# Two tiles of a fused attention and MLP kernel transposed by DMA instead of TensorE, and placed two or three slots sooner

## The chip, the cores and the metric

The kernel runs on one core of a Trainium2 chip. The metric is the device time of one execution in microseconds (us). The kernel before takes 292.99 us (median of 3 runs, 292.66 to 293.11).

## The reference

A linear attention with a normalisation per head, followed by an MLP with layer norm and a residual. B = 8 batches, H = 8 heads, S = 576 positions, D = 64, model width 512, hidden width 2048:

```
kv  = einsum('bhsd,bhse->bhde', k, v)
o   = einsum('bhsd,bhde->bhse', q, kv)
x   = o / sqrt(mean(o*o, -1) + 1e-6) * g_norm          # then heads side by side: (B, S, 512)
xn  = (x - mean(x)) / sqrt(var(x) + 1e-6) * g_ln
out = x + relu(xn @ w_ch1) @ w_ch2
```

## The kernel before: the parts that matter

Each batch has four main tiles of 128 positions, and a remainder of 64 positions that is paired with the next batch's. One tile passes through `o` (TensorE, product with kv), `sq` (ScalarE, squares), `red` (VectorE, the reduction that sums the squares of each head), the root (ScalarE), `y`, `x` and `xc` (VectorE: normalise, scale, centre), `var` (ScalarE) and `turn`, which gives the transposed `xT` that the first MLP product reads:

```python
def turn(self, on_pe):
    dst = self.blk[2][:, :, self.ts * 128:(self.ts + 1) * 128]
    if on_pe:
        tp = ps_m.tile([128, nK, 128], bf16, tag="misc", name="tp")
        for kk in range(nK):                                  # 4 transposes on TensorE
            nc.tensor.transpose(tp[:, kk, :], self.xc_t[:, kk * 128:(kk + 1) * 128], identity)
        nc.scalar.copy(dst, tp)                               # and a copy on ScalarE
    else:
        nc.sync.dma_start_transpose(dst, self.xc_t)           # one DMA on SP's queue
    ...
```

The MLP products of earlier batches run on TensorE, and the tiles of later batches are put between them at fixed places, called slots. A slot is four hidden blocks of MLP work for one tile (or as much for several), about 0.9 us. It is a place in the program order of every engine, not a moment in time:

```python
def plan_tile(s, make, turn_at, on_pe):
    ...                            # first(): o, sq, red;   second(): root, y, x, xc
    at(s, first)                   # third(): var;          fourth(): turn(on_pe)
    at(s + 2, second)
    at(s + 6, third)
    at(turn_at, fourth)
```

Batch 2, which the change touches, and the later batches:

```python
at(36, lambda: kv_of(2))
at(36.5, lambda: turn_q_dma(2))
for j, s, tn in ((0, 46, 53), (1, 51, 58), (2, 55, 63), (3, 59, 68)):
    plan_tile(s, lambda j=j: main_tile(2, j), tn, True)
plan_tile(62, lambda: rem_tile(1), 69, False)
...
for b in range(3, B):
    s = 32 * b
    ...                                                 # load_batch(b), gated on qt of b - 1
    d = -41 if b == 3 else -45
    at(s + d, lambda b=b: kv_of(b))
    at(s + d + 1.7, lambda b=b: turn_q_dma(b))          # q_p copy on VectorE, then qt by DMA on SP
    for j in range(J):
        o = s + d + (10 if b == 3 else 12) + 5 * j
        plan_tile(o, lambda b=b, j=j: main_tile(b, j), o + 6, False)
    ...
```

Slots 48 to 63 are the second MLP product of batch 1, with an output store on SP after every fourth slot. Slots 64 to 71 are the first MLP product of batch 2 for its tiles 0 and 1, slots 72 to 79 for tiles 2 and 3. So `xT` of tiles 0 and 1 is needed at slot 64 and that of tiles 2 and 3 at slot 72. Tile 0 of batch 3 has its `o` at slot 65 and needs `qt` of batch 3, the transposed queries, by then.

Of the kernel before, what the change touches and what calls it, by code (L numbers as in the profile page):

```python
# [14 lines left out]
def kernel(  # L15
# [183 lines left out]
    def turn_q_dma(b):  # L199
        q_p = kv_in.tile([128, JJ, H, D], bf16, tag="qp", bufs=2)  # L200
        nc.vector.tensor_copy(q_p.rearrange("p j h d -> p h j d"), q_in[b % NB])
        q_t = qt_pool.tile([128, JJ, HP, 128], bf16, tag="qt", name="qt")
        nc.sync.dma_start_transpose(
            q_t.rearrange("p j hp t -> p (j hp) t"), q_p.rearrange("p j h d -> p (j h d)"))
        qts[b] = q_t
# [35 lines left out]
    def new_block(n, bufs):  # L241
        x_blk = xpool.tile([128, 4, Dm], f32, tag=f"x{n}", bufs=bufs, name="x_blk")
        st_blk = xpool.tile([128, 3, 4], f32, tag=f"st{n}", bufs=bufs, name="st_blk")
        xT_blk = xpool.tile([128, nK, 512], bf16, tag=f"xT{n}", bufs=bufs, name="xT_blk")
        return x_blk, st_blk, xT_blk
# [98 lines left out]
    def main_tile(b, j, pool=None, tag="ops"):  # L344
        q_t, kvp = qts[b], held[b]
        if b not in blks:
            blks[b] = new_block("main", 3)
        return Tile([(slice(0, 128), lambda hp: q_t[:, j, hp, :], kvp)], blks[b], j, pool, tag)

    def rem_tile(b):  # L350
        mms = []
        for half, bb in enumerate((b - 1, b)):
            qt, kp = qts.pop(bb), held.pop(bb)
            mms.append((slice(half * 64, (half + 1) * 64),
                        lambda hp, qt=qt: qt[:, J, hp, :64], kp))
        if "rem" not in blks:
            blks["rem"] = new_block("rem", 1)
        return Tile(mms, blks["rem"], b // 2)

    def plan_tile(s, make, turn_at, on_pe):  # L360
        box = []

        def first():
            t = make()
            box.append(t)
            t.o()
            t.sq()
            t.red()

        def second():  # L370
            t = box[0]
            t.y()
            t.x()
            t.xc()

        def third():
            box[0].var()

        def fourth():
            box[0].turn(on_pe)  # L380

        at(s, first)
# [3 lines that stand above are left out]
# [72 lines left out]
    def at(slot, fn):  # L458
        agenda.setdefault(int(slot), []).append((slot, fn))
# [145 lines left out]

    at(36, lambda: kv_of(2))
    at(36.5, lambda: turn_q_dma(2))
    for j, s, tn in ((0, 46, 53), (1, 51, 58), (2, 55, 63), (3, 59, 68)):
        plan_tile(s, lambda j=j: main_tile(2, j), tn, True)
    plan_tile(62, lambda: rem_tile(1), 69, False)  # L610
    at(78, lambda: rstd_of(2))

    for b in range(3, B):
        s = 32 * b
# [69 lines left out]
```

## Time and profile before

| what | value | view |
|---|---|---|
| time, median | 292.99 us | timed runs |
| span of the profiled execution | 291.4 us | page |
| PE busy | 283.4 us, 97% | page, part 1 |
| PE busy from 90 to 93 us | 2.73 of 3.00 us | table of windows |
| PE weight loads waiting for qt of batches 4 to 7 | 2.0 us in 4 waits | view of waits |

First the head of the page of before: busy time, share and number of instructions of TensorE's products (PE) and of its weight loads (PEld).

```profile
span 291.4 us, 5801 instructions
PE 283.4 (97%) x2320; PEld 159.1 (55%) x2320; DVE 150.7 (52%) x335; ACT 154.7 (53%) x341; POOL 41.9 (14%) x68
```

TensorE bounds the kernel. Next, windows of before: the window's length, then busy time of PE, PEld, DVE, ACT and POOL (with numbers of instructions), the granted clock, the DMA share and GB/s.

```profile
63.00:66.00 3.00, 3.00 (x57) 3.00 (x55) 0.04 (x1) 2.26 (x6) 2.87 (x5) 1.00 0.49 50
81.00:84.00 3.00, 3.00 (x27) 1.80 (x27) 2.86 (x8) 1.18 (x2) 0.98 (x2) 1.00 0.90 178
87.00:90.00 3.00, 3.00 (x34) 2.72 (x33) 2.49 (x5) 2.15 (x7) 1.06 (x2) 1.00 1.31 217
90.00:93.00 3.00, 2.73 (x26) 2.30 (x24) 1.79 (x5) 3.00 (x9) 0.00 (x0) 1.00 1.39 189
```

VectorE has nothing to do from 63 to 66 us (0.04 us) and is nearly full near 81 to 84 us. TensorE has one hole in this stretch, after 90 us. The timeline of before (start, duration, engine, line, operation, and in brackets the idle time before it and what ended it) shows where the hole comes from. It also has the rows that later distances start and end at: the last transpose of batch 1, which I use as a mark, the `o` of the third tile of batch 3, and the last output operation. `p` is an MLP product in PSUM, the memory that TensorE writes to; `m` is ScalarE's eviction of it, which frees that part of PSUM (a bank) for the next product.

```profile
61.15 0.39 PE L337 MATMUL tp<-identity,xc 128*128 128x128 bf16 x4
76.55 0.82 DVE L201 COPY q_p<-q_in 128x2560 bf16<-128x2560 bf16 x1
77.86 3.18 SPq L203 DMA_TRANSPOSE qt<-q_p  x1
84.30 0.39 PE L260 MATMUL o_ps<-kv_pack,qt 128*128 128x128 bf16 x4
...
87.42 0.68 DVE L287 TENSOR_REDUCE ss<-sq 128x8 f32<-128x512 f32 x1
88.13 0.30 ACT L297 ACTIVATE rms<-ss,eps_sb 128x8 f32<-128x8 f32 x1 [0.85 <-DVE ss L287]
88.34 0.58 ACT L405 ACTIVATE m<-p 128x512 bf16<-128x512 f32 x1
...
90.00 1.08 ACT L405 ACTIVATE m<-p 128x512 bf16<-128x512 f32 x2
90.64 3.68 PE L402 MATMUL p<-xT_blk,w_sb 128*128 128x256 bf16 x32 [0.27 <-ACT m L405]
94.16 0.39 PE L260 MATMUL o_ps<-kv_pack,qt 128*128 128x128 bf16 x4
...
287.90 0.35 DVE L423 SCALAR_TENSOR_TENSOR o_sb<-p,rstd,x_blk 128x128 f32<-128x128 f32 x1 [0.54 <-PE p L418]
```

Read it backwards. TensorE stops at 90.6 us because ScalarE has not yet emptied a PSUM bank (`m` at 90.00). ScalarE had stood idle for 0.85 us until 88.13 behind a root, waiting for the reduction at 87.42; the eviction at 88.34 comes after that root in program order and ran after it, though the last matmul of its product ended at 87.30 in the timeline (87.03 + 0.27). That reduction began 3.1 us after the `o` of its tile (at 84.30), since VectorE had a backlog (it is busy without a pause from 84.22 us, with outputs and the work of earlier tiles).

Last, from the view of waits and the source view of before: the waits on qt, and the time that the DMA transposes of a tile's `xT` take from issue to landing (all data arrived).

```profile
PEld L260 <- DMA qt<-q_p: 2.0, 4, 0.6
...
L341 SPq DMA_TRANSPOSE xT_blk<-xc x24: 1189/1216/1365, 87.5 to 227.9; - x24
...
DMA to landing us min/median/max: 2.4/3.5/9.1
```

A DMA turn occupies SP for 1.2 us and lands after 2.4 us at best, 9.1 at worst.

### The profile page before, as it was taken

What the parts mean: (1) busy time and instruction counts of PE and PEld (TensorE: products, weight loads), DVE (VectorE), ACT (ScalarE), POOL (GpSimd) and SP (SyncE); (2) the same over time, 40 slices, a digit from 0 to 9 for tenths busy, and PEclk for the clock granted to TensorE, in tenths of its full rate; (3) what the DMA queues carried; (4) which work ended last, traced back from release to release, by engine and by line L of the source; (5) the groups of instructions that cost most, each with busy time, mean ns of one, the idle gap of its engine ahead of it and who ended that gap; (6) DMA issues with size and microseconds to landing.
All of it is one profiled execution on the core that took longest, in us unless ns stands there. A gap on an engine that the chain in (4) does not pass through costs nothing.

```text
span 291.4 us, 5801 instructions
## 1 busy us (share of the span) xinstructions
PE 283.4 (97%) x2320; PEld 159.1 (55%) x2320; DVE 150.7 (52%) x335; ACT 154.7 (53%) x341; POOL 41.9 (14%) x68
## 2 busy tenths in 40 slices
PE   8889999999999999999999999999999999999995
PEld 3579755995578654444444444444444444444444
DVE  5776028836996893765266936752678200220022
ACT  3457755885569931882189408920894066016500
POOL 8522520032050003200220023000000000000000
PEclk9999999999999999999999999999999999999999
DMA  7999999469789818993999279939202510131033
GB/s 212 202 206 205 198 204 217 102 100 192 144 141 201 110 41 153 217 162 65 159 192 140 56 145 192 165 64 167 58 18 55 109 36 0 38 78 30 0 74 72
DMA packets 63290, 35.84 MB, mean 123 GB/s; under 512 B 30748, under 2 KB 58268, under 8 KB 63264
## 3 DMA queue, kind: packets, MB, share of 16 engines
q0 software_dynamic: 28016, 17.76, 43.8%
q1 hardware_dynamic: 34736, 16.99, 29.7%
q10 hardware_dynamic: 512, 0.72, 0.8%
q8 instruction: 18, 0.29, 0.4%
q14 instruction: 8, 0.07, 0.1%
HBM read 36.71 MB, written 9.44 MB: 158 GB/s over the span
## 4 chain that ended last, share of the span: by engine, by line
PE 83%; DMA 6%; DVE 6%; ACT 2%; issue 1%; POOL 1%; POOLq 0%
PE p L402 40%; PE p L418 36%; DMA qt<-q_p 4%; PE o_ps L260 3%; DMA q_in<-in_q_dram 2%; PE kv_ps L235 2%; DVE ss L287 1%; DVE x_blk L311 1%; DVE y L292 1%; DVE o_sb L423 1%; PE tp L183 1%; ACT m L405 1%; PE p L196 1%; ACT xT_blk L339 1%; PE tp L337 0%
## 5 line engine op out<-in xcount | busy, mean ns | idle before, releaser
L402 PE MATMUL p<-xT_blk,w_sb 128*128 128x128 bf16 (+2 forms) x1024 | 132.0, 286 | 0.5 <-ACT m L405 0.3
L418 PE MATMUL p<-w_sb,m 128*128 128x512 bf16 (+2 forms) x608 | 130.2, 368 | 0.0
L405 ACT ACTIVATE m<-p 128x512 bf16<-128x512 f32 x144 | 85.2, 597 | 45.3 <-PE p L402 43.5
L402 PEld LDWEIGHTS <-w_sb 128*128 128x128 bf16 x1024 | 78.6, 98 | 45.5 <-issue 1.1
L418 PEld LDWEIGHTS <-m 128*128 128x128 bf16 x608 | 56.6, 98 | 60.3
L423 DVE SCALAR_TENSOR_TENSOR o_sb<-p,rstd,x_blk 128x512 f32<-128x512 f32 (+2 forms) x38 | 27.3, 719 | 44.2 <-PE p L418 41.5
L266 ACT ACTIVATE sq<-o_ps 128x512 f32<-128x512 f32 x34 | 20.2, 595 | 38.9 <-PE o_ps L260 38.9
L287 DVE TENSOR_REDUCE ss<-sq 128x8 f32<-128x512 f32 x34 | 23.2, 682 | 19.8 <-ACT sq L266 19.8
L329 ACT ACTIVATE dev<-x_blk,st_blk 128x512 f32<-128x512 f32 x36 | 25.8, 718 | 6.2 <-DVE st_blk L315 6.1
L321 DVE SCALAR_TENSOR_TENSOR xc<-x_blk,st_blk,g_ln_sb 128x512 bf16<-128x512 f32 x34 | 25.6, 752 | 1.2
L292 DVE TENSOR_TENSOR y<-o_ps,inv 128x512 f32<-128x512 f32 x34 | 23.5, 691 | 2.6
L311 DVE SCALAR_TENSOR_TENSOR x_blk<-y,g_norm_sb 128x512 f32<-128x512 f32 x34 | 23.5, 691 | 1.2
L411 DVE RECIPROCAL rstd<-rstd 128x4 f32<-128x4 f32 x9 | 1.6, 174 | 39.3 <-ACT rstd L410 39.3
L304 DVE RECIPROCAL inv<-rms 128x8 f32<-128x8 f32 x36 | 7.2, 200 | 22.5 <-ACT rms L297 22.4
L98 POOL COPY gate<-qt 1x1 bf16<-1x1 bf16 x5 | 1.4, 287 | 115.3 <-DMA qt<-q_p 115.3
L297 ACT ACTIVATE rms<-ss,eps_sb 128x8 f32<-128x8 f32 x36 | 10.8, 300 | 7.8 <-DVE ss L287 7.1
L260 PEld LDWEIGHTS <-qt 128*128 128x128 bf16 (+1 forms) x152 | 9.7, 100 | 8.4 <-DMA qt<-q_p 2.0
L260 PE MATMUL o_ps<-kv_pack,qt 128*128 128x128 bf16 (+1 forms) x152 | 13.3, 221 | 0.4 <-DVE qt L191 0.2
L196 PE MATMUL p<-fill_sb 128*128 128x512 bf16 x28 | 8.6, 465 | 1.2 <-DVE eps_sb L137 1.2
L339 ACT COPY xT_blk<-tp 128x512 bf16<-128x512 bf16 x10 | 5.8, 579 | 2.3 <-PE tp L337 2.3
L329 ACT ACTIVATION_READ_ACCUMULATOR dev<-x_blk,st_blk 128x1 f32 x36 | 7.0, 193 | 0.0
L238 ACT CAST kv_pack<-kv_ps 64x256 bf16<-64x256 f32 x7 | 2.6, 365 | 7.9 <-PE kv_ps L235 7.8
(79 smaller groups left out, 119.0 us busy)
## 6 DMA issues: line engine op xcount, KB each, us to landing
out_dram<-o_sb SPq DMA_DIRECT2D x70, 128.0 KB, 2.5
w_sb<-in_moe_w_ch_dram POOLq DMA_DIRECT2D x8, 512.0 KB, 13.8
k_in<-in_k_dram POOLq DMA_DIRECT2D x7, 320.0 KB, 5.1
v_in<-in_v_dram POOLq DMA_DIRECT2D x7, 320.0 KB, 8.8
q_in<-in_q_dram POOLq DMA_DIRECT2D x7, 320.0 KB, 12.1
q_in<-in_q_dram POOLq DMA_DIRECT2D x8, 256.0 KB, 12.4
k_in<-in_k_dram POOLq DMA_DIRECT2D x7, 256.0 KB, 6.5
v_in<-in_v_dram POOLq DMA_DIRECT2D x7, 256.0 KB, 11.0
```

The source lines that it names most:

```text
L196: nc.tensor.matmul(p1, lhsT=fill_sb[:, :128], rhs=fill_sb, start=True, stop=True)
L260: nc.tensor.matmul(flat[rows, hp * 128:(hp + 1) * 128], lhsT=lhsT_of(hp), rhs=kvp[:, hp, :], start=True, stop=True)
L266: nc.scalar.activation(self.sq_t, self.o_ps, func=AF.Square)
L287: nc.vector.tensor_reduce(self.ss, self.sq_t, axis=AX.X, op=ALU.add)
L292: nc.vector.tensor_mul(self.y_t, self.o_ps, self.inv().to_broadcast([128, H, D]))
L311: nc.vector.scalar_tensor_tensor(x_blk[:, ts].rearrange("p (h d) -> p h d", h=H), in0=self.y_t, scalar=1.0, in1=g_norm_sb.to_broadcast([12 ...
L321: nc.vector.scalar_tensor_tensor(self.xc_t, in0=x_blk[:, self.ts], scalar=st[:, 1, self.ts:self.ts + 1], in1=g_ln_sb, op0=ALU.add, op1=ALU ...
L329: nc.scalar.activation(dev, x_blk[:, ts], func=AF.Square, bias=st[:, 1, ts:ts + 1], accum_out=st[:, 2, ts:ts + 1])
L402: nc.tensor.matmul(p1[:, i, :], lhsT=w1_sb[:, kk, de * 128:(de + 1) * 128], rhs=blk[2][:, kk, sl], start=(kk == 0), stop=(kk == nK - 1))
L405: nc.scalar.activation(m1[:, de0:de0 + per, sl], p1, func=AF.Relu)
L418: nc.tensor.matmul(p2[:, c0:c1], lhsT=m1s[b][:, de, ts * 128:(ts + 1) * 128], rhs=w2_sb[:, de, c0:c1], start=(de == 0), stop=(de == nDe - 1))
L423: nc.vector.scalar_tensor_tensor(o_sb[:, c0:c1], in0=p2[:, c0:c1], scalar=rstds[b][:, ts:ts + 1], in1=blks[b][0][:, ts, c0:c1], op0=ALU.mu ...
```

## The change

The intent is to take eight transposes off TensorE, which bounds the kernel, and to start tiles 0 and 1 earlier so that the longer way of a DMA turn still ends before slot 64.

```diff
-    for j, s, tn in ((0, 46, 53), (1, 51, 58), (2, 55, 63), (3, 59, 68)):
-        plan_tile(s, lambda j=j: main_tile(2, j), tn, True)
+    for j, s, tn in ((0, 44, 50), (1, 48, 54), (2, 53, 61), (3, 58, 67)):
+        plan_tile(s, lambda j=j: main_tile(2, j), tn, j > 1)
```

Tiles 2 and 3 stay on TensorE, but they too move by two slots and one slot.

## The prediction

> **What bounds the kernel now.** TensorE. The profile's first part has PE busy 283.4 us of 291.4 (97%), and the chain of waits is 83% PE. The change acts from 63 to 91 us. In the table of 3 us windows PE is full there but for 90 to 93 us (2.73 of 3.00). The wait view names that hole: PE waited 0.3 us for ScalarE's `m` eviction. The chain explains it backwards: ScalarE sat 0.85 us behind a root that needed `red` of the remainder tile, late because VectorE had been backed up since about 73 us (2.9 of 3 us busy in most windows from 69 to 87).
>
> **What it removes.** For tiles 0 and 1: 4 transposes each, 0.22 us of PE per tile in the chain (0.45 us together, on the critical engine), and two ScalarE copies of 0.58 us, off the chain.
>
> **What it adds.** Two DMA transposes on SP's queue: 1.2 us of issue each; the 24 present ones land after 2.4 us alone, 7 to 9 us beside batch loads (source view). Even 9 us is in time: I expect xc of tile 0 at about 69 us and of tile 1 at 73, xT by 76 to 79; slot 64 starts at 83.
>
> **What it moves.** Tile 0 goes from slot 46 to 44 (about 63.2 us; qt landed at 62.6, so no wait), tile 1 from 51 to 48, tile 2 from 55 to 53, tile 3 by one. VectorE starts where it was idle (0.04 of 3 us in 63 to 66). But its order changes: y, x, xc of tile 2 (2.5 us) now precede output 1 of batch 1 and the q_p copy of batch 3, and the reductions are followed at once by the root they wait for (some 0.5 us exposed each time). I estimate that q_p starts at 77.5 to 78 instead of 76.55. Its DMA transpose (5.0 us to landing, 83.0 before) then lands at about 84.0; slot 65 needs it at 83.8 (before 84.2). So a new PE wait of 0 to 0.5 us on qt of batch 3 is likely.
>
> Second collision: the transposes share DMA engines with the loads of batch 3 (k and v landed by 72.2, q by 75.4). The Trainium skill, page "DMA: Bandwidth & Descriptors", section "Issuing engines are not separate DMA queues", says DMAs of all issuers run on the same 16 engines and interleave; the trace agrees (7.8 us against 2.4 to landing). One tile is about 1 us of all engines (estimate from the queue shares); kv of batch 3 needs v at 73.55: slack 1.3 us, so 0 to 0.3 us of PE wait.
>
> **Sum.** -0.45 (PE transposes), -0.1 to -0.3 (the hole at 90.6 shrinks), +0.25 (qt), +0.05 (v): net about -0.3 us. After 95 us PE order drives the kernel, so what is gained stays; the four later waits on qt (2.0 us together) remain.
>
> Predicted 292.65 us, 8 in 10 between 292.0 and 293.4. Chances: faster by over 2% 0.01, within 2% 0.98, slower by over 2% 0.01.
>
> **What would show it.** Right: 32 PE transposes of xc instead of 40, 26 DMA transposes of xT; PE busy about 0.5 us less; slot 64 about 0.4 us earlier; q_p of batch 3 about 1 us later and a new short PE wait on qt near 84 us; the hole at 90.6 smaller. Wrong: PE waiting for xT at slot 64, for kv inputs near 73.5, or for a PSUM bank held by a late output near 79.
>
> **What would make it wrong.** Transposes slowing the loads more than estimated; VectorE's backlog growing, so that qt comes over 1 us late and later loads follow; or VectorE keeping up, so that the whole 0.7 us is kept.

## The result, and the profile after

The new kernel takes 292.48 us (median of 4 runs, 292.22 to 292.58) against 293.01 us for before (292.66 to 293.11, 4 runs, three of them those above). The ratio is 0.9983, with a 95% interval of 0.9965 to 1.0000. Ratios here are the mean time of one kernel's runs over that of the other's in the same rounds, so they are not quite the ratio of the medians quoted.

The same views of the new kernel, first the head of its page:

```profile
span 290.8 us, 5789 instructions
PE 283.6 (98%) x2312; PEld 158.6 (55%) x2312; DVE 151.0 (52%) x335; ACT 154.1 (53%) x339; POOL 41.3 (14%) x68
```

There are eight products and eight weight loads fewer, and two ScalarE copies fewer. PE busy is nevertheless not smaller (283.6 against 283.4 us): among other differences, the warm-up products at the start of the kernel, which the change does not touch, show 9.4 us against 8.6. The time of the weight loads fell, 159.1 to 158.6 us. Then the windows of the new kernel:

```profile
63.00:66.00 3.00, 3.00 (x58) 3.00 (x56) 0.69 (x1) 2.52 (x7) 2.99 (x5) 1.00 0.53 51
81.00:84.00 3.00, 2.97 (x25) 1.59 (x20) 2.65 (x8) 1.64 (x5) 0.00 (x0) 1.00 1.06 199
87.00:90.00 3.00, 3.00 (x32) 2.70 (x31) 2.36 (x6) 3.00 (x8) 2.07 (x4) 1.00 1.24 156
90.00:93.00 3.00, 3.00 (x30) 2.69 (x28) 1.60 (x4) 2.83 (x8) 0.00 (x0) 1.00 1.49 141
```

The hole after 90 us is gone, and a small one has appeared in 81 to 84 us (2.97). The timeline of the new kernel says what it is:

```profile
61.06 0.39 PE L337 MATMUL tp<-identity,xc 128*128 128x128 bf16 x4
...
69.02 1.20 SPq L341 DMA_TRANSPOSE xT_blk<-xc  x1
74.53 2.33 SPq L341 DMA_TRANSPOSE xT_blk<-xc  x1
77.57 0.82 DVE L201 COPY q_p<-q_in 128x2560 bf16<-128x2560 bf16 x1
78.89 3.25 SPq L203 DMA_TRANSPOSE qt<-q_p  x1
83.94 0.23 PEld L260 LDWEIGHTS <-qt 128*128 128x128 bf16 x4 [0.31 <-DMA qt<-q_p]
86.30 0.68 DVE L287 TENSOR_REDUCE ss<-sq 128x8 f32<-128x512 f32 x1
87.09 0.31 ACT L297 ACTIVATE rms<-ss,eps_sb 128x8 f32<-128x8 f32 x1
93.36 0.39 PE L260 MATMUL o_ps<-kv_pack,qt 128*128 128x128 bf16 x4
...
287.42 0.35 DVE L423 SCALAR_TENSOR_TENSOR o_sb<-p,rstd,x_blk 128x128 f32<-128x128 f32 x1 [0.54 <-PE p L418]
```

The q_p copy of batch 3 starts 1.0 us later than in before, its transpose is issued 1.0 us later, and at 83.94 us TensorE waits for it: a wait that before did not have. (The ends of products are modelled, so the window shows little of it; but that `o` follows the first product of slot 64 by 1.07 us, against 0.88 in before.) The reduction of tile 0 of batch 3 starts at 86.30 us instead of 87.42, and the root that had held ScalarE back now runs at 87.09 with no idle time ahead of it. From the view of waits and the source view of the new kernel:

```profile
PEld L260 <- DMA qt<-q_p: 2.3, 4, 1.0
...
L341 SPq DMA_TRANSPOSE xT_blk<-xc x26: 1189/1199/2358, 69.0 to 227.9; - x26
```

**Measuring against a mark.** The start of the kernel scatters from run to run: the mark stands at 61.15 us in before and at 61.06 in the new kernel, and among all profiled runs it lies between 60.71 and 62.16. (The latest, in dma_only, goes with a granted clock of 0.89 from 15 to 30 us, where before has 1.00; after the mark it has 1.00 too.) The code up to the mark is the same in all of them. I therefore count from the mark. The third tile's `o` of batch 3 comes 33.01 us after it in before (94.16 - 61.15) and 32.30 us after it in the new kernel (93.36 - 61.06): a lead of 0.71 us. At the end of the kernel (start of the last output operation) the distances are 226.75 and 226.36 us, so only 0.39 us of the lead is left. The rest of the 0.5 us between the medians is not accounted for by the stretch after the mark; it lies within the scatter of the timed runs.

### The profile page after: what moved, and what is told of

It is laid out like the page before. It is cut to its first block, busy times and chain, and to the rows that moved or that the text cites. A ratio compares the mean times of both kernels' runs of the same rounds, so it can differ in the third digit from the quotient of the medians. Undisturbed runs are those within 1.5% of the kernel's fastest.

```text
span 290.8 us, 5789 instructions
## 1 busy us (share of the span) xinstructions
PE 283.6 (98%) x2312; PEld 158.6 (55%) x2312; DVE 151.0 (52%) x335; ACT 154.1 (53%) x339; POOL 41.3 (14%) x68
## 4 chain that ended last, share of the span: by engine, by line
PE 89%; DMA 6%; ACT 1%; DVE 1%; issue 1%; POOL 1%; POOLq 0%
PE p L402 42%; PE p L418 39%; DMA qt<-q_p 4%; PE o_ps L260 3%; DMA q_in<-in_q_dram 2%; PE kv_ps L235 2%; PE tp L183 1%; PE p L196 1%; PE tp L337 1%; ACT sq L266 0%; PE tp L170 0%; POOL v_in L126 0%; PE o_half L500 0%; ACT xT_blk L542 0%; ACT m L405 0%
## 5 line engine op out<-in xcount | busy, mean ns | idle before, releaser
L196 PE MATMUL p<-fill_sb 128*128 128x512 bf16 x28 | 9.4, 501 | 1.2 <-DVE eps_sb L137 1.2
L196 PEld LDWEIGHTS <-fill_sb 128*128 128x128 bf16 x28 | 3.2, 121 | 6.1 <-issue 3.9
```

The source lines that it names most:

```text
L196: nc.tensor.matmul(p1, lhsT=fill_sb[:, :128], rhs=fill_sb, start=True, stop=True)
```

## The experiments

**Theory.** Two separate terms make the lead: 0.45 us of TensorE transposes removed, and the hole near 90 us, which closes because VectorE starts earlier. Two things take part of it back: the new wait on qt of batch 3 and the later waits on qt. **Rivals.** The hole closed because ScalarE has two copies fewer, or because of the DMA turns; or there is one term only; or the result is noise.

All twelve runs gave correct results, and each is "same" as before at 2%. Distances are from the mark in the profiled execution. "Slot 64" is the first product of batch 2's MLP, "o(3,2)" the third tile's `o` of batch 3. The medians come from four jobs, in which before had 293.01, 292.78, 293.18 and 292.94 us.

| kernel | slot 64 | o(3,2) | last output | median us (job) |
|---|---|---|---|---|
| before | 22.27 | 33.01 | 226.75 | 293.01 (1) |
| new kernel | 21.82 | 32.30 | 226.36 | 292.48 (1) |
| after_again | 21.82 | 32.30 | 226.37 | 292.41 (3) |
| shift_only | 22.27 | 32.55 | 226.46 | 292.57 (2) |
| dma_only | 22.05 | 32.50 | 226.59 | 292.64 (2) |
| slack3 | 21.83 | 32.10 | 226.16 | 292.24 (2) |
| before_slack3 | 22.26 | 32.54 | 226.35 | 292.38 (3) |
| slack_all | 21.82 | 32.10 | 225.12 | 291.44 (2) |
| slack_all_b | 21.82 | 32.10 | 225.13 | 291.61 (4) |
| before_slack_all | 22.27 | 32.55 | 225.57 | 291.75 (3) |
| before_slack_all_b | 22.27 | 32.55 | 225.57 | 291.71 (4) |
| slack_all_t2 | 21.60 | 31.87 | 224.90 | 291.43 (3) |
| after_t2 | 21.60 | 32.30 | 225.66 | 291.84 (4) |
| slack_all_t23 | 21.60 | 38.30 | 231.42 | 298.32 (4) |

Three kernels were profiled twice (the new one and the two with slack throughout), and their distances agree within 0.01 us. That is why these columns can carry differences of 0.2 us and the timed medians can't. Before itself was profiled once.

### after_again: is the first result noise?

No edit; the new kernel once more.

> The new kernel itself, beside the others of this call. Theory: 0.4 to 0.6 us under before, as at first (0.53 us), and in the trace TensorE is 0.6 to 0.8 us ahead of before at the o product of the third tile of batch 3 (near 94 us), counted from the transpose of the last tile of batch 1, with 0.1 to 0.4 us of it given back at the later waits on qt. Rival (the first result was noise): within 0.15 us of before.

It took 292.41 us (292.28 to 292.72, 6 runs) against 293.18 (292.56 to 294.57, 11 runs), ratio 0.9978 (0.9963 to 0.9992). The median difference of 0.77 us is above the expected range, because before scattered upwards in this job: two of its eleven runs, at 294.00 and 294.57 us, show a lower mean clock, 0.994; without them its median is 292.97 and the difference 0.56 us. The trace is the same as the first within 0.01 us at both ends: a lead of 0.71 us at o(3,2), of which 0.33 us is lost by the end. The noise rival falls.

### shift_only: the new slots, all turns on TensorE

The tiles stand as in the new kernel; the turns of tiles 0 and 1 are one and three slots later than there.

```diff
-    for j, s, tn in ((0, 44, 50), (1, 48, 54), (2, 53, 61), (3, 58, 67)):
-        plan_tile(s, lambda j=j: main_tile(2, j), tn, j > 1)
+    for j, s, tn in ((0, 44, 51), (1, 48, 57), (2, 53, 61), (3, 58, 67)):
+        plan_tile(s, lambda j=j: main_tile(2, j), tn, True)
```

> The slots of the new kernel, but all four tiles of batch 2 turned on TensorE (40 transposes of xc, as before). Theory (the gain is two terms: 0.45 us of TensorE transposes removed by the DMA turns, and 0.45 us of a TensorE stop near 90 us that goes because VectorE's work on batch 2 starts 2 us sooner): the stop near 90 us is gone here as well, TensorE reaches slot 65 about 0.45 us later than in the new kernel and so does not wait for qt of batch 3 (landing near 84.0), and the time is about 0.3 to 0.5 us under before, within 0.2 us of the new kernel. Rival (ScalarE's two freed copies, or the DMA turns themselves, removed the stop): the stop of 0.3 us or more near 90 us stays, and the time equals before within 0.15 us.

292.57 us, ratio to before 0.9988 (0.9976 to 1.0000). Slot 64 comes exactly where it does in before (22.27), since no TensorE work is removed, and o(3,2) comes 0.46 us sooner. The hole is gone and there is no wait on qt at slot 65:

```profile
90.00:93.00 3.00, 3.00 (x30) 2.70 (x28) 1.70 (x4) 2.84 (x8) 0.00 (x0) 1.00 1.32 182
```

So the shift alone closes the hole, with all of ScalarE's copies kept, and the hole is worth 0.46 us. (The shift also moves tile 3's copy one slot forward, from behind the root to ahead of it. That this is not what closes the hole is shown by before_slack3, where no copy changes its slot.) The timed median lies 0.21 us under before, less than the expected 0.3 to 0.5; the trace's end, 0.29 us under before, has the same order.

### dma_only: the old slots, tiles 0 and 1 turned by DMA

```diff
-    for j, s, tn in ((0, 44, 50), (1, 48, 54), (2, 53, 61), (3, 58, 67)):
+    for j, s, tn in ((0, 46, 53), (1, 51, 58), (2, 55, 63), (3, 59, 68)):
         plan_tile(s, lambda j=j: main_tile(2, j), tn, j > 1)
```

> The slots of before, tiles 0 and 1 turned by DMA. Theory: tile 1's turn now stands on SP behind the 640 KB transpose of batch 3 (issue until about 81.1 us), so its xT lands at 84 to 86 us while slot 64 needs it at about 83.0: TensorE waits 1 to 3 us there, and the time is 0.3 to 2 us above before. The shift is thus needed for the DMA turn. Rival (a DMA turn needs no head start; its only effect is 0.45 us less TensorE work): no wait at slot 64, and the time is 0.4 us under before.

A miss: I expected 0.3 to 2 us above before, and the time equals that of before. It took 292.64 us (292.35 to 293.95; the profiled run is the slowest), ratio 0.9999 (0.9983 to 1.0014). Tile 1's transpose did stand behind that of batch 3 on SP, until 81.6 us, but landed 2.5 us later. The chain of waits of this run has the transpose, and its timeline the weight loads of slot 64:

```profile
81.64 2.53 DMA xT_blk<-xc
...
84.22 0.75 PEld L402 LDWEIGHTS <-w_sb 128*128 128x128 bf16 x7 [0.35 <-issue]
```

Slot 64 comes at 22.05 us instead of 21.82 in the new kernel: a wait of 0.23 us, not of 1 to 3. The chain passes through this DMA, which lands at 84.17 us, just before the weight loads go on; the label "issue" in the line above only says that the timeline found no releaser. I had taken the long landings beside batch loads for the rule; here the loads of batch 3 had landed and those of batch 4 had not begun. At slot 64 the head start is worth 0.23 us, no more. The hole near 90 us shrank to 0.15 us in the weight loads (0.45 in before) without the shift; TensorE came to it later by the wait at slot 64, so the two effects are mixed in this run, and it does not tell how the hole depends on the copies.

### before_slack3: only the hole's cause

Before, with tile 0 of batch 3 one slot later and nothing else.

```diff
-            o = s + d + (10 if b == 3 else 12) + 5 * j
+            o = s + d + (10 if b == 3 else 12) + 5 * j + (b == 3 and j == 0)
```

> The kernel before, with tile 0 of batch 3 one slot later and nothing else. There is no wait on qt of batch 3 to remove in before. Theory (the TensorE stop near 90.6 us comes from ScalarE standing behind the root of that tile, whose reduction VectorE's backlog delays to 88.1 us): in program order the root now comes after four more products, so fewer evictions stand behind it, the stop falls from 0.45 us to under 0.15 us and TensorE is 0.3 to 0.5 us ahead of before near 95 us. Rival (the stop comes from ScalarE's xT copies or its load in general): the stop stays at 0.3 us or more, and the time equals before within 0.15 us.

292.38 us against 293.18, ratio 0.9979 (0.9964 to 0.9994), about as fast as the new kernel without any of its change. The lead at o(3,2) is 0.47 us. Its windows:

```profile
87.00:90.00 3.00, 3.00 (x33) 2.71 (x31) 1.62 (x5) 3.00 (x8) 0.55 (x1) 1.00 1.30 229
90.00:93.00 3.00, 3.00 (x30) 2.70 (x28) 2.46 (x7) 2.88 (x8) 0.00 (x0) 1.00 1.36 183
```

ScalarE is full from 87 to 90 us (2.15 of 3 in before), TensorE has no hole. The number of copies is that of before. So the hole was one instruction in the wrong place of ScalarE's program order: a root placed ahead of evictions while its input was still behind VectorE's backlog. The edit moves all of that tile's work by a slot; that it was the root is read from the traces (0.85 us of idle time before it in before, none here). Either moving the tile later or clearing the backlog sooner (shift_only) closes the hole.

### slack3: the new wait on qt of batch 3

The same edit, applied to the new kernel.

> The new kernel with tile 0 of batch 3 one slot (0.9 us) later, so that qt of batch 3 has landed. Theory: the wait of 0.31 us that the trace shows on qt near 84 us goes, TensorE reaches 95 us about 0.2 us sooner, and the time is 0.1 to 0.25 us under the new kernel, if nothing gives it back at the later waits on qt. Rival (the wait costs nothing, later waits take it back): the same time within 0.1 us.

292.24 us (292.10 to 292.38), ratio to before 0.9976 (0.9964 to 0.9988), against 292.48 and 292.41 us for the new kernel in the other jobs. o(3,2) comes 0.20 us sooner than in the new kernel, and the last output as well (226.16 against 226.36). The wait of 0.31 us in the weight loads cost 0.20 us of TensorE time, and nothing later took that back.

### slack_all and before_slack_all: all waits on qt taken away

```diff
-            o = s + d + (10 if b == 3 else 12) + 5 * j
+            o = s + d + (10 if b == 3 else 12) + 5 * j + (j == 0)
```

> The new kernel with tile 0 of every batch from 3 to 7 one slot later. The new kernel's trace has 2.3 us of TensorE waits on qt (0.31, 0.64, 0.99, 0.35 and none at 202 us). Theory: these waits are on the chain, since the tile is placed about one slot before its qt lands; they go, and the time falls by 1.2 to 2.2 us to 290.3 to 291.3. Rival (qt is tied to TensorE's progress through VectorE's order, or the tile's later start makes a new wait at its first product): 0.5 us or less.

> The kernel before, with tile 0 of every batch from 3 to 7 one slot later. The four waits on qt (2.0 us in the trace of before) go. Theory: 1.2 to 2.0 us under before; and against the new kernel with the same slack (291.44 us in the last call) it is 0.4 to 0.6 us slower: that is what the DMA turns save in TensorE work (0.45 us) when neither the stop near 90 us nor the waits on qt hide it. Rival (the change's gain is only the stop's removal): within 0.15 us of the new kernel with slack.

> The new kernel with one slot of slack for tile 0 of batches 3 to 7, again, beside the kernel before with the same slack. Theory (two TensorE turns cost 0.45 us, and nothing hides it once there are no waits on qt): 0.35 to 0.6 us under the kernel before with slack, and its span, counted from the last transpose of batch 1, 0.45 to 0.6 us shorter. Rival (the DMA turns save nothing by themselves, the gain was the stop near 90 us): within 0.15 us.

> The partner of the run before it: the kernel before with the same slack. Theory: 0.35 to 0.6 us over it, no stop near 90 us, no wait on qt, the time 291.6 to 292.0. Rival: within 0.15 us of it.

In none of the four traces does TensorE wait on qt. The new kernel with slack takes 291.44 and 291.61 us, ratios to before 0.9954 (0.9941 to 0.9967) and 0.9957 (0.9937 to 0.9977); before with slack takes 291.75 and 291.71 us, ratios 0.9953 (0.9938 to 0.9968) and 0.9953 (0.9939 to 0.9967). For the new kernel the fall is 0.8 to 1.0 us, short of the 1.2 that I expected; its distance to the last output falls by 1.24 us. Before with slack falls by 1.43 and 1.23 us, as expected, and its distance by 1.18.

Between the two kernels with slack, the distance to the last output differs by 0.45 us in one pair and 0.44 in the other, as expected and as at slot 64 (22.27 - 21.82). So two DMA turns save 0.45 us, and with no waits on qt all of it arrives at the end. The shift adds nothing more there, since the slack has already closed the hole: at o(3,2) the two differ by the same 0.45 us. The timed medians of the shared job differ by only 0.10 us, which misses the expected 0.35 to 0.6; over both jobs they are 291.48 (11 runs) and 291.72 (12 runs). The saving is shown by the traces; the timed runs don't resolve it.

### after_t2: where 0.3 us of the lead went

The new kernel loses 0.3 us between o(3,2) and the end. The chain of waits of before and of the new kernel each has the transpose of batch 5. Before:

```profile
136.91 6.20 DMA qt<-q_p
```

New kernel:

```profile
136.17 6.58 DMA qt<-q_p
```

In most places this transpose lands 4.8 to 5.1 us after its issue, but in these two kernels one or two of them are slow: in before those of batch 5 and batch 7 (6.2 and 6.1 us), in the new kernel that of batch 5 alone (6.6 us; batch 7 has 4.9). The weight loads wait 0.61 and 0.48 us for these two batches in before, and 0.99 and 0 us in the new kernel. The lead follows: at the first `o` of batches 4, 5, 6 and 7, counted from the mark, the new kernel is 0.65, 0.28, 0.25 and 0.39 us ahead of before. Batch 5 costs 0.37 us of it, and batch 7 gives 0.14 back. All runs with two DMA turns show the second pattern of landings, with slack or without (batch 5 at 6.5 to 6.6 us, batch 7 at 4.9); all runs with none show the slow landing in batch 7 (6.1 to 6.4 us). shift_only has the pattern of before and dma_only that of the new kernel, so it goes with the turns and not with the slots of the tiles. To tell "TensorE is ahead, so it waits more" from "the slow landing moves with the number of transposes in the queue", I sent one more transpose:

```diff
-        plan_tile(s, lambda j=j: main_tile(2, j), tn, j > 1)
+        plan_tile(s, lambda j=j: main_tile(2, j), tn, j > 2)
```

> The new kernel without slack, with tile 2 of batch 2 turned by DMA as well: one more transpose on SP's queue. In the traces so far the transposes of batches 5 and 7 landed after 6.2 and 6.1 us with all turns on TensorE, after 6.6 and 4.9 us with two DMA turns (0.99 us of wait in batch 5), and after 4.8 and 4.9 us with three. Theory (a slow landing whose place depends on how many transposes went through the queue decides how much of the lead is given back): the wait on qt of batch 5 falls from 0.99 us to under 0.6 us, and the time is 0.4 to 0.9 us under the new kernel (292.4): 0.22 us of TensorE work and the smaller wait. Rival (the wait in batch 5 belongs to TensorE being ahead): it stays at 0.9 us or grows, and the time is at most 0.25 us lower.

291.84 us (291.75 to 292.29), ratio to before 0.9959 (0.9945 to 0.9974). From the waits of this run, and the source view of its transpose of batch 5:

```profile
PEld L260 <- DMA qt<-q_p: 1.5, 3, 0.6
...
DMA to landing us min/median/max: 4.9/4.9/4.9
```

The transpose of batch 5 lands after 4.9 us and its wait is gone. At o(3,2) this kernel stands exactly with the new one (32.30): TensorE is 0.22 us earlier at slot 64 and gives that back at the wait on qt of batch 3, now 0.53 us. It ends 0.70 us sooner (225.66 against 226.36), and 0.66 of this is there at the first `o` of batch 5 (81.07 us from the mark against 81.73). So the rival falls: the wait in batch 5 is not owed to TensorE's lead. What makes one transpose slow at a place that depends on how many went before it is not shown by these runs.

### slack_all_t2 and slack_all_t23: why tiles 2 and 3 were left on TensorE

To the new kernel with slack, `j > 2` in the first; in the second, all four by DMA, with tile 3's turn at slot 64:

```diff
-    for j, s, tn in ((0, 44, 50), (1, 48, 54), (2, 53, 61), (3, 58, 67)):
-        plan_tile(s, lambda j=j: main_tile(2, j), tn, j > 1)
+    for j, s, tn in ((0, 44, 50), (1, 48, 54), (2, 53, 61), (3, 58, 64)):
+        plan_tile(s, lambda j=j: main_tile(2, j), tn, False)
```

> The new kernel with the slack of one slot for all batches, and tile 2 of batch 2 turned by DMA too, at slot 61. Its turn stands on SP behind the transpose of batch 3 and two stores, is issued near 83.4 us and shares the DMA engines with the loads of batch 4. Theory: it lands in 4 to 8 us, 87.5 to 91.5 us, while slot 72 needs it at 89.5: TensorE waits 0 to 2 us there, and the saved 0.22 us is lost: 0 to 1.5 us over the same kernel with tile 2 on TensorE (291.44). Rival (a DMA turn is safe there too): 0.2 us under it, no wait at slot 72.

> The new kernel with slack, and tiles 2 and 3 of batch 2 turned by DMA too (slots 61 and 64). Tile 3's transpose is issued near 84.6 us, beside the first loads of batch 4. Theory: it lands 4 to 8 us later, near 89 to 92.5 us, slot 72 needs it at 89.3 us: TensorE waits 0.3 to 3 us there, so the time is 0 to 2.5 us over the kernel with slack (291.44) and tile 3 must stay on TensorE. Rival (the turn is safe): 0.4 us under it.

slack_all_t2 takes 291.43 us (291.35 to 292.04), ratio to before 0.9946 (0.9931 to 0.9961). There is no wait at slot 72, and the last output comes 0.22 us sooner than in slack_all (224.90 against 225.12): the rival was right, tile 2 can be turned by DMA as well. By the traces it is the fastest kernel; the timed median equals that of slack_all in another job.

slack_all_t23 takes 298.32 us (297.48 to 298.73), ratio 1.0173 (1.0153 to 1.0192). The direction was expected, the size was not. From its waits and its chain:

```profile
PE p L402 <- DMA xT_blk<-xc: 5.2, 1, 5.2
...
85.78 9.32 DMA xT_blk<-xc
```

Tile 3's transpose was issued at 85.78 us, after two output stores on SP and 1.4 us after the loads of batch 4 had begun, and took 9.3 us to land. Tile 2's, issued at 83.17 us before those loads, took 2.5 us. TensorE stood for 5.2 us. The lead lost is larger, 6.43 us at o(3,2) (38.30 against 31.87 in slack_all_t2), because TensorE came back slower: the granted clock is 1.00 while it stands from 90 to 94 us, 0.50 from 95 to 97 and 1.00 again from 98 to 99, and the 24 products after the wait take 4.10 us instead of the 2.78 of as many in before. With its turn at this place, tile 3 must stay on TensorE.

## Why the prediction was right, and where its steps were off

The predicted time, 292.65 us, lies 0.17 us over the measured one, the range held it, and each of the main steps can be checked. (Before alone had medians from 292.78 to 293.18 us in the four jobs, so the agreement of the times says little; the steps are checked in the traces.)

- **PE transposes, -0.45 us: right.** Slot 64 comes 0.45 us sooner from the mark (22.27 to 21.82), and not at all sooner in shift_only.
- **The q_p copy of batch 3 at 77.5 to 78 us, a new wait of 0 to 0.5 us on qt: right.** It starts at 77.57 us, and the wait of 0.31 us in the weight loads cost 0.20 us, shown by slack3. It was put at +0.25.
- **`xT` by 76 to 79 us, in time for slot 64: right.** The two DMA turns, issued at 69.02 and 74.53 us, landed after 7.3 and 3.9 us, that is, at 76.3 and 78.4 us, and slot 64 starts at 82.88.
- **The wait on v, +0.05 us: none.** kv of batch 3 starts at 73.45 us with no wait on a load, and v took 6.6 and 7.2 us to land (6.6 and 7.3 in before). The first DMA turn, issued at 69.02, did not delay it. The q loads behind it took 9.1 and 10.3 us instead of 8.3 and 9.0, and the turn itself 7.3 us, against 2.4 at best in before, so the sharing that the Trainium skill describes ("DMA: Bandwidth & Descriptors", "Issuing engines are not separate DMA queues") is there: it fell on transfers that were not awaited. In slack_all_t23 it fell on one that was: 9.3 us beside the loads of batch 4, against 2.5.
- **The hole near 90 us, -0.1 to -0.3: mis-sized.** It closed completely and was worth 0.46 us (shift_only), 0.47 us (before_slack3). The prediction also named the wrong tile: it said "`red` of the remainder tile"; the reduction is that of tile 0 of batch 3.
- **"After 95 us PE order drives the kernel, so what is gained stays": the step that failed.** The lead was 0.71 us at o(3,2) and 0.39 us at the end. The later waits on qt again sum to 2.0 us in the weight loads (0.64, 0.99 and 0.35, against 0.58, 0.61, 0.31 and 0.48), as foretold, but they lie elsewhere and cost TensorE more: 0.37 us of the lead is gone after batch 5, whose transpose lands after 6.6 us, and 0.14 comes back at batch 7. after_t2 shows that this depends on which transpose lands slowly.
- **"PE busy about 0.5 us less": a sign that could not show it.** It rose by 0.2 us. The Trainium skill ("Perfetto Trace Analysis", "Identifying the Most-Contended Engine") warns that matmul busy time is no measure of the distance to the roofline, and points to the busy time of weight loads. That fits here: it fell from 159.1 to 158.6 us.

The sum held because two errors met: the hole gave about 0.25 us more than predicted, and the later waits took back about 0.3 us that the prediction had not counted. That the two nearly cancel is luck. What the runs settle is a chain of amounts: 0.45 us (transposes) + 0.46 us (hole) - 0.20 us (new wait on qt) = 0.71 us, and then 0.32 us lost at the later waits. What stays open is what makes some transposes land 1.2 to 1.7 us later than the others.

## What to carry to other kernels

Work taken off the bounding engine counts only if that engine doesn't stand at its next wait: of the 0.91 us that this change gained (0.45 + 0.46), 0.52 went to waits on a transpose, and one slot of slack at those waits was worth more (1.24 us in the traces of the new kernel) than the whole change (0.39 us). When an in-order engine is both a consumer of a slow chain and the one that empties PSUM, look at what stands ahead of the evictions in its program order; one tile placed a single slot too soon, and with it one such operation, cost 0.46 us. For changes below 0.3%, compare traces from a common mark after the scattered start, and repeat one of them to know how far the distances can be trusted.

## What the Trainium skill lacked or had wrong

- "DMA: Bandwidth & Descriptors", "Latency and other measured facts", gives 261 GB/s and more as the effective bandwidth of a DMA transpose. Its table does not say what the queue pays (the page has cycle counts of the issuing sequencer, but in its part on trn3 and not for such sizes): here the issue on SP mostly takes 1.2 us for 128 KB and 3.1 us for 640 KB, during which nothing else on that queue is issued, and from issue to landing they take 2.4 and 4.9 us alone, that is, about 55 and 134 GB/s (131072 and 655360 bytes over these times).
- The section "Issuing engines are not separate DMA queues" of that page says that DMAs interleave, but has no figure for what this does to a small DMA: a 128 KB transpose took 2.5 us when issued just before a batch's loads began and 9.3 us when issued 1.4 us after (slack_all_t23).
- I found no page with the slow transposes: 6.1 to 6.6 us instead of 4.9 for the same 640 KB, at a place that moved from batches 5 and 7 to batch 5 alone, and then to neither of them, with 0, 2 and 3 more transposes on the queue before it (before, the new kernel, after_t2).
